# The last list products in a bank of their own, the last sums one place later, and the expert lists in two steps

## The chip, the cores and the metric

One NeuronCore of a Trainium2 chip runs the whole kernel. The metric is the device time in microseconds (us). The kernel before takes 431.78 us, the median of three runs (431.11 to 434.26).

## The reference

The input is a sliding-window attention and the output a mixture of experts on top of it.

```python
# attention: q, k, v of 8 x 8 x 576 x 64, window 64, causal
scores = where(0 <= rel < 64, q @ k.T / 8, -1e9)
x = softmax(scores) @ v          # as 4608 tokens x 512
# mixture of 8 experts, each 512 -> 1024 -> 512
do_compute = x @ w_skip > 0      # the others pass through unchanged
logits = xc @ w_gate             # xc = x[do_compute]
e = argmax(logits); gate = softmax(logits)[e]
out = x;  out[do_compute] = xc + gate * (relu(xc @ w1[e]) @ w2[e])
```

About half the tokens are computed, each by one expert. All arithmetic is in 32-bit floats: matmuls split each operand into a high and a low part and add three products (high x high, and the two mixed ones).

## The kernel before, in words

**The attention part.** The 4608 tokens are 36 tiles of 128. For each tile TensorE makes the scores, VectorE and ScalarE the softmax, TensorE transposes and multiplies by `v`. The logits come out of the same product. `tile_out` (line 782) ends a tile.

**Routing.** Tiles are gathered into five groups (`GRP`, 8, 8, 6, 6 and 8 tiles). For each group the generator `route` (line 507) finds each token's expert, as a one-hot (`gohb`), and its place in that expert's list: the matmuls of lines 515 and 518 make prefix sums in the PSUM tile `pr`, and line 528 adds the running `base`. Then the generator `enter` (line 540) writes the tokens into the lists by matmuls too: `one_hots` (line 576) makes, for each tile, a one-hot of the place inside a list block (`at`, line 601) and a weighted one-hot of the block (line 609), and line 558 multiplies them into `lp`, which line 563 adds to `found`. After the last group `last_entries` (line 672) orders the lists by the size of the experts: a multiplication (line 682) and a sum (line 689) each for the token numbers (c = 0) and the gates (c = 1), then line 691 makes the indices `les`.

**The order of the work** is written by hand, and every engine works its instructions off in that order. Two queues of generators, `late` (of `route`) and `later` (of `enter`), advance by one step at each call of `routes` (line 761). A generator says "sums" ahead of the prefix sums and "lists" ahead of the list products. Behind the last attention tile (`progress[0] == NT`) these steps are held for a number of calls, `HOLD`, so that what they wait for is ready.

**The expert part.** Tokens are worked off in nine items of up to 400 rows, the experts by size. The first two items were gathered early. `expert_chunks` (line 1050) issues a half step of an item at each turn: `up` (product `p`, its high part `hh` by ScalarE, its low part `hl` by VectorE, in two PSUM banks that alternate), and two steps later `down` (into `yw`, `yv` or `yu`). Between them `split_x` (line 879) transposes the next item's rows into the tile `px` and splits them into `xh` and `xl`. `weights_to` (line 850) loads pieces of 512 KB into six buffers (`raw`) and splits them into a high part (`whi`, ScalarE) and a low part (`wlo`, VectorE, line 844), into a ring of nine slots. While routing is not done, it splits only what is needed next; later one piece more at each turn (line 1204).

**The handover.** Behind the last attention tile each turn is: a half step of the experts (`expert_chunk`), one call of `routes`, and, once the last sums are added, one step of `order_experts` (line 1233), which ranks the experts by size. When both queues are empty, each turn may also gather the rows of a further item by POOL's indirect transfers (line 730).

**PSUM banks in the handover.** The pool `late` has four banks: one under the tag "g", two under "w" and one under "u". `pr`, the last `lp` tiles and the `px` tiles all share "g", so each of them waits until the one before it has been read. The bank "u" is used for the first time by the `down` of the fourth item.

Of the kernel before, what the change touches and what calls it, by code (L numbers as in the profile page):

```python
# [8 lines left out]
F32 = mybir.dt.float32  # L9
# [4 lines left out]
ALU = mybir.AluOpType  # L14
# [5 lines left out]
N, D, E, F = 4608, 512, 8, 1024  # L20
P = 128
NB = S // 64
NT = N // P
# [17 lines left out]
NCLOSE = 22  # L41
# [3 lines left out]
NL = E * LT  # L45
# [13 lines left out]
BOTH = 20  # L59
WAIT = {28: 6}  # L60
LWAIT = 8
HOLD = {"sums": 2, "lists": 2}

NXG = 9
CLOSED = 4 * S + 512
# [76 lines left out]
def window_attention_moe(ctx: ExitStack, tc, a, out):  # L142
    nc = tc.nc
# [12 lines left out]
    lists = dram.tile([LROWS, 2], I32, name="lists")  # L156
# [131 lines left out]
    banks = {}  # L288
# [251 lines left out]
    def enter(t0, n):  # L540
        yield
        while t0 >= NCLOSE and progress[0] < NT:
            yield
        parts = [one_hots(t0, n)]
        if t0 + n == NCLOSE:
            parts.insert(0, close_first())
        while parts:
            parts = [z for z in parts if next(z, z) is not z]
            if parts:
                yield  # L550
        at, one = made[0]
        yield "lists"
        if progress[0] < NT:
            lp = banks["av"][:, 0, LAT : LAT + 5 * NL]
        else:
            lp = banks["late"].tile([P, 5 * NL], F32, name="lp", tag="g", bufs=1, padded_shape=[P, 512])
        for j in range(n):
            nc.tensor.matmul(
                lp, at[:, j], one[j // 4][:, j % 4], start=j == 0, stop=j == n - 1, skip_group_check=True
            )  # L560
        yield "listed"
        flat = found.rearrange("p v e j -> p (v e j)")
        nc.vector.tensor_tensor(flat, flat, lp, op=ALU.add)
        if t0 + n == NCLOSE:
            for _ in first_entries():
                yield
            while stores:
                store()
            side.extend(
                (gather_x, xgs[j], es0[:, 0, j // 2, j % 2 : j % 2 + 1], CLOSED) for j in range(4)  # L570
            )
        if t0 + n == NT:
            for _ in last_entries():
                yield

    def one_hots(t0, n):
        g = nc.gpsimd
        here = rows[:, t0 : t0 + n]
        of = xgs[5][:, : n * NL].rearrange("p (n a) -> p n a", a=NL)
        at = xgs[8].bitcast(BF16)[:, : n * P].rearrange("p (n k) -> p n k", k=P)  # L580
        one = [xgs[6 + z].bitcast(BF16)[:, : 4 * 5 * NL].rearrange("p (n v a) -> p n v a", v=5, a=NL) for z in range(2)]
        c = sm.tile([P, n], F32, name="gc")
        g.tensor_scalar(c, here, 1.0 / P, (P / 2 - 0.5) / P, op0=ALU.mult, op1=ALU.subtract)
        g.tensor_scalar(c, c, ROUND, None, op0=ALU.add)
        g.tensor_scalar(c, c, ROUND, float(P), op0=ALU.subtract, op1=ALU.mult)
        k = sm.tile([P, n], F32, name="gk")
        g.tensor_tensor(k, here, c, op=ALU.subtract)
        left = ent[:, t0 : t0 + n, 1]
        for v in (2, 3, 4):
            g.tensor_copy(vals[:, t0 : t0 + n, v], left)  # L590
            if v < 4:
                r = sm.tile([P, n], F32, name=f"gl{v}")
                g.tensor_tensor(r, left, vals[:, t0 : t0 + n, v], op=ALU.subtract)
                left = r
        yield
        tab = cf[:, off["tab"]].unsqueeze(1).to_broadcast([P, n, NL])
        g.tensor_tensor(of, tab, c.unsqueeze(2).to_broadcast([P, n, NL]), op=ALU.subtract)
        g.tensor_scalar(of, of, 0.0, None, op0=ALU.is_equal)
        by = g if t0 < NCLOSE else nc.vector
        for j in range(n):  # L600
            by.tensor_scalar(at[:, j], cf[:, off["iota"]], k[:, j : j + 1], None, op0=ALU.is_equal)
        yield
        for z in range(2):
            m = min(4, n - 4 * z)
            if m > 0:
                r = slice(4 * z, 4 * z + m)
                dims = [P, m, 5, NL]
                v5 = vals[:, t0 + 4 * z : t0 + 4 * z + m]
                g.tensor_tensor(
                    one[z][:, :m], of[:, r].unsqueeze(2).to_broadcast(dims), v5.unsqueeze(3).to_broadcast(dims),  # L610
                    op=ALU.mult,
                )
        made[0] = at, [z.rearrange("p n v a -> p n (v a)") for z in one]
        yield
# [3 lines left out]
    def close_first():  # L618
        g = nc.gpsimd
        key = sm.tile([P, E], F32, name="ckey", bufs=1)  # L620
        cmp = xgs[4][:, : E * E].rearrange("p (i j) -> p i j", i=E)
        rank = sm.tile([P, E], F32, name="crank", bufs=1)
        t1 = sm.tile([P, E], F32, name="ct1", bufs=1)
        g.tensor_scalar(key, base, 16.0, None, op0=ALU.mult)
        g.tensor_tensor(key, key, cf[:, off["kc"]], op=ALU.add)
        g.tensor_tensor(
            cmp,
            key.unsqueeze(1).to_broadcast([P, E, E]),
            key.unsqueeze(2).to_broadcast([P, E, E]),
            op=ALU.subtract,  # L630
        )
        yield
        g.tensor_scalar(cmp, cmp, 0.0, None, op0=ALU.is_gt)
        add_up(rank, cmp, E)
        for j in range(2):
            g.tensor_scalar(first[:, j], rank, float(j), None, op0=ALU.is_equal)
        g.tensor_scalar(t1, rank, 1.5, None, op0=ALU.is_lt)
        g.tensor_tensor(t1, t1, cf[:, off["full"]], op=ALU.mult)
        g.tensor_tensor(t1, t1, base, op=ALU.subtract)
        g.tensor_scalar(t1, t1, 0.0, None, op0=ALU.max)  # L640
        g.tensor_tensor(base, base, t1, op=ALU.add)
        yield
        pl = cmp[:, 0:2]
        m1 = sm.tile([P, 2], F32, name="cm1", bufs=1)
        g.tensor_tensor(pl, first, cf[:, off["e8"]].unsqueeze(1).to_broadcast([P, 2, E]), op=ALU.mult)
        add_up(m1, pl, E)
        g.tensor_scalar(perm, m1, float(NQ * P), None, op0=ALU.mult)
        tables["closed"] = True
# [8 lines left out]
    def first_entries():  # L657
        both = sm.tile([P, 2, E, 2], F32, name="cboth", bufs=1)
        put_together(both, 0, 2)
        yield  # L660
        mine = sm.tile([P, 2, 2, E], F32, name="cmine", bufs=1)
        got = sm.tile([P, 2, 2, 2], F32, name="cgot", bufs=1)
        dims = [P, 2, 2, E]
        for r in range(2):
            is_r = first[:, r].unsqueeze(1).unsqueeze(1).to_broadcast(dims)
            nc.gpsimd.tensor_tensor(mine, both.rearrange("p c e j -> p c j e"), is_r, op=ALU.mult)
            add_up(got[:, r], mine, E)
            yield
        nc.gpsimd.tensor_scalar(es0[:, 0], got[:, :, 0], float(N), None, op0=ALU.add)
        nc.gpsimd.tensor_copy(es0[:, 1].bitcast(F32), got[:, :, 1])  # L670

    def last_entries():
        both = xgs[5][:, : 2 * NL].rearrange("p (c e j) -> p c e j", c=2, j=LT)
        put_together(both, 0, LT)
        yield
        while "order" not in tables:
            yield
        dims = [P, E, LT, E]
        mine = tables["mine"]
        got = tables["got"]  # L680
        for c in range(2):
            nc.vector.tensor_tensor(
                mine,
                both[:, c].rearrange("p e j -> p j e").unsqueeze(1).to_broadcast(dims),
                tables["is"].unsqueeze(2).to_broadcast(dims),
                op=ALU.mult,
            )
            yield
            nc.vector.tensor_reduce(got[:, c], mine, axis=AX.X, op=ALU.add)
            yield  # L690
        nc.vector.tensor_scalar(tables["lists"], got[:, 0], float(N), None, op0=ALU.add)
        for i in range(2, len(ITEMS)):
            its[i].lists(tables["lists"], got[:, 1], ITEMS[i][0], CAP // P if ITEMS[i][0] < 2 else 0)

# [56 lines left out]
    late = []  # L751

    later = []
    held, held2 = [None, 0], [None, 0]
# [6 lines left out]
    def routes(n):  # L761

        for _ in range(n):
            for queue, h in ((late, held), (later, held2)):
                if not queue:
                    continue
                if h[0] in ("sums", "lists"):
                    h[1] += 1
                    if progress[0] < NT or h[1] < HOLD[h[0]] or held[0] == "added":
                        continue  # L770
                step(queue, h)

# [24 lines left out]
    progress = [0]  # L797
# [68 lines left out]
    tables = {}  # L866
# [562 lines left out]
```

## Time and profile before

| | us |
|---|---|
| median of three runs | 431.78 |
| the profiled execution | 432.43 |
| its span in the trace | 430.6 |
| TensorE (PE) busy | 399.1 (93%) |
| VectorE (DVE) busy | 291.2 (68%) |
| ScalarE (ACT) busy | 219.4 (51%) |
| GpSimd (POOL) busy | 157.2 (36%) |

The busy time of an engine counts each of its instructions from start to end, those that overlap once. [...] An idle time stands in brackets behind an instruction, with the instruction that ended it. The handover from attention to experts is at about 160 to 193 us.

### The profile page before, as it was taken

Reading aid. Unit: us, or ns where it says so; the run is one execution under the profiler, and the core shown is the slowest. Engines: PE = TensorE matmul, PEld = TensorE weight load, DVE = VectorE, ACT = ScalarE, POOL = GpSimd, SP = SyncE. Lnnn points to the kernel's source line nnn. Section 1 sums busy time; section 2 is a strip of 40 time slices with the busy share of each in tenths; the row PEclk is TensorE's granted clock in tenths of the full one; section 3 lists DMA queues with packets and bytes.
Section 4 is the critical chain, followed back from the end, with each engine's and each line's share of the span. In section 5 each row is a group of like instructions: output and inputs, shape, how many; then the busy total and the mean of one; then the engine's idle time right before and its main releaser. Section 6 shows DMA issues by size and latency. Waiting matters only on the chain.

```text
span 430.6 us, 11760 instructions
## 1 busy us (share of the span) xinstructions
PE 399.1 (93%) x4673; PEld 330.5 (77%) x4673; DVE 291.2 (68%) x513; ACT 219.4 (51%) x388; POOL 157.2 (36%) x298
## 2 busy tenths in 40 slices
PE   5898999999998977779999899999999999999983
PEld 3576878777786867769898688898887789888662
DVE  3487999889798878779435589475374576756540
ACT  0676787777667675226233445244253444444520
POOL 5211359549679786614304024032043030101011
PEclk9999999999999999899999999999999999999998
DMA  8999999999995984345737827455578675659400
GB/s 271 409 324 329 406 363 376 402 379 294 395 413 158 323 306 149 129 164 187 277 123 243 279 101 266 165 171 179 173 231 279 215 245 193 220 178 300 150 34 20
DMA packets 38840, 105.71 MB, mean 246 GB/s; under 512 B 4896, under 2 KB 6816, under 8 KB 38784
## 3 DMA queue, kind: packets, MB, share of 16 engines
q1 hardware_dynamic: 34160, 93.51, 63.3%
q0 software_dynamic: 3200, 9.58, 6.1%
q10 hardware_dynamic: 1424, 1.85, 1.2%
q8 instruction: 37, 0.61, 0.5%
q14 instruction: 19, 0.16, 0.1%
HBM read 90.86 MB, written 14.39 MB: 244 GB/s over the span
## 4 chain that ended last, share of the span: by engine, by line
PE 76%; DMA 10%; DVE 7%; ACT 3%; POOL 2%; issue 1%; SPq 1%; ACTq 0%; DVEq 0%; POOLq 0%
PE p L908 9%; PE p L910 8%; PE p L909 8%; PE av L386 7%; PE pt L283 6%; PE ps L250 4%; PE yv L908 4%; PE yv L910 3%; PE yv L909 3%; PE yw L908 3%; PE yw L910 3%; DMA vt<-vpt 3%; PE yw L909 3%; DMA q<-qT 3%; DVE wlo L844 2%; PE pw L334 2%
## 5 line engine op out<-in xcount | busy, mean ns | idle before, releaser
L844 DVE TENSOR_TENSOR wlo<-raw,whi 128x1024 fp32r<-128x1024 f32 x70 | 86.2, 1239 | 15.9 <-ACT whi L840 14.0
L954 ACT ACTIVATE hh<-p 128x256 fp32r<-128x256 f32 (+6 forms) x72 | 27.7, 385 | 134.1 <-PE p L910 132.2
L908 PE MATMUL p<-xh,whi 128*128 128x256 f32 (+6 forms) x288 | 85.8, 298 | 0.2 <-ACT xh L886 0.2
L909 PE MATMUL p<-xl,whi 128*128 128x256 f32 (+6 forms) x288 | 84.2, 293 | 0.9 <-DVE xl L889 0.9
L910 PE MATMUL p<-xh,wlo 128*128 128x256 f32 (+6 forms) x288 | 84.2, 292 | 0.0
L957 DVE SCALAR_TENSOR_TENSOR hl<-p,hh 128x256 fp32r<-128x256 f32 (+6 forms) x72 | 30.3, 421 | 67.6 <-ACT hh L954 35.3
L840 ACT CAST whi<-raw 128x1024 fp32r<-128x1024 f32 x72 | 74.5, 1046 | 0.0
L992 POOL DMA_INDIRECT out<-yo,les x18 | 17.6, 976 | 154.6 <-DVE yo L991 151.8
L908 PEld LDWEIGHTS p<-xh,whi 128*128 128x128 f32 x288 | 55.3, 192 | 3.5 <-issue 1.0
L909 PEld LDWEIGHTS p<-xl,whi 128*128 128x128 f32 x288 | 55.3, 192 | 2.2 <-DVE xl L889 1.2
L910 PEld LDWEIGHTS p<-xh,wlo 128*128 128x128 f32 x288 | 55.3, 192 | 0.0
L275 ACT ACTIVATE s<-s 128x1024 f32<-128x1024 f32 x36 | 38.1, 1059 | 25.6 <-DVE s L270 25.5
L269 DVE TENSOR_REDUCE mx<-ps 128x8 f32<-128x1024 f32 x36 | 43.6, 1212 | 8.1 <-PE ps L250 8.1
L270 DVE TENSOR_TENSOR s<-ps,mx 128x1024 f32<-128x1024 f32 x36 | 44.1, 1225 | 5.0 <-ACT vt L371 0.5
L386 PEld LDWEIGHTS av<-vm,ptm 128*64 128x64 f32 x992 | 34.6, 136 | 11.4 <-issue 4.5
L386 PE MATMUL av<-vm,ptm 128*64 128x74 f32 x992 | 39.6, 231 | 2.5 <-POOL vm L355 1.4
L284 ACT COPY ptm<-pt 128x512 f32<-128x512 f32 x72 | 38.2, 581 | 5.7 <-PE pt L283 5.4
L283 PE MATMUL pt<-ident,s 128*128 128x128 f32 x288 | 39.2, 279 | 0.5 <-issue 0.5
L250 PE MATMUL ps<-k,q 64*64 64x128 f32 x1024 | 35.2, 274 | 3.1 <-DMA q<-qT 3.0
L250 PEld LDWEIGHTS ps<-k,q 64*64 64x64 f32 x1024 | 30.9, 136 | 7.0 <-DMA q<-qT 3.4
L283 PEld LDWEIGHTS pt<-ident,s 128*128 128x128 f32 x288 | 30.9, 141 | 3.1 <-issue 0.8
L355 POOL COPY vm<-vm 64x1184 f32<-64x1184 f32 x16 | 18.7, 1166 | 32.1 <-ACT vm L354 28.6
(224 smaller groups left out, 693.9 us busy)
## 6 DMA issues: line engine op xcount, KB each, us to landing
raw<-wq SPq DMA_DIRECT2D x72, 512.0 KB
vm<-vp SPq DMA_DIRECT2D x15, 592.0 KB
vT<-vT SPq DMA_DIRECT2D x16, 512.0 KB
out<-x SPq DMA_DIRECT2D x32, 256.0 KB
q<-qT SPq DMA_DIRECT2D x14, 512.0 KB
wr<-wq SPq DMA_DIRECT2D x24, 256.0 KB
k<-kT SPq DMA_DIRECT2D x7, 640.0 KB
k<-kT SPq DMA_DIRECT2D x7, 512.0 KB
```

What stands on the lines that cost most here:

```text
L250: nc.tensor.matmul(ps[64 * hf : 64 * hf + 64, r, p], q[h, p], k[h, :, p], start=False, stop=p == 3, skip_group_check=True,)
L269: nc.vector.tensor_reduce(mx, flat, axis=AX.X, op=ALU.max)
L270: pace[0] = nc.vector.tensor_tensor(s, flat, mx.unsqueeze(2).to_broadcast([P, 8, P]), op=ALU.subtract)
L275: nc.scalar.activation(s, s, AF.Exp, scale=0.125)
L283: nc.tensor.transpose(pt[:, p], s[:, 4 * r + p], ident)
L284: nc.scalar.copy(ptm[:, 4 * r : 4 * r + 4], pt)
L386: nc.tensor.matmul(av[64 * hf : 64 * hf + 64, h // 4, (h % 4) * VW : (h % 4 + 1) * VW], ptm[:, (h % 2) * 4 + h // 2, 64 * hf : 64 * hf + 6 ...
L840: nc.scalar.copy(ring[n % RING][0], raws[n % NRAW])
L844: by.tensor_tensor(lo, raws[n % NRAW], hi.bitcast(F32), op=ALU.subtract)
L908: nc.tensor.matmul(o, lh, rh, start=first, stop=False)
L909: nc.tensor.matmul(o, lh, rl, start=False, stop=False)
L910: nc.tensor.matmul(o, ll, rh, start=False, stop=last)
```

## The change

`HOLD` for the sums becomes 3. The hold on the lists no longer asks whether the sums have been issued and not added; it lasts one call longer while a route is in the queue `late`. The last `lp` tiles take the tag "u". In `one_hots` the choice of the engine moves into the loop. In `last_entries` the token numbers (c = 0) are multiplied, summed and turned into indices in one step, the gates in the next, where there were five steps.

```diff
-HOLD = {"sums": 2, "lists": 2}
+HOLD = {"sums": 3, "lists": 2}
...
-            lp = banks["late"].tile([P, 5 * NL], F32, name="lp", tag="g", bufs=1, padded_shape=[P, 512])
+            lp = banks["late"].tile([P, 5 * NL], F32, name="lp", tag="u", bufs=1, padded_shape=[P, 512])
...
-        by = g if t0 < NCLOSE else nc.vector
         for j in range(n):
+            by = g if t0 < NCLOSE else nc.vector
             by.tensor_scalar(at[:, j], cf[:, off["iota"]], k[:, j : j + 1], None, op0=ALU.is_equal)
...
-            yield
             nc.vector.tensor_reduce(got[:, c], mine, axis=AX.X, op=ALU.add)
-            yield
-        nc.vector.tensor_scalar(tables["lists"], got[:, 0], float(N), None, op0=ALU.add)
+            if c == 0:
+                nc.vector.tensor_scalar(tables["lists"], got[:, 0], float(N), None, op0=ALU.add)
+                yield
...
-                    if progress[0] < NT or h[1] < HOLD[h[0]] or held[0] == "added":
+                    if progress[0] < NT or h[1] < HOLD[h[0]] + (h is held2 and len(late)):
```

## Rows read from the trace of the kernel before

**Rows 1.** Busy time by stretches: us, each engine's busy us (instructions), clock, DMA share, GB/s.
```profile
160.00:193.00 33.00, 26.04 (x223) 23.73 (x220) 26.26 (x66) 12.17 (x22) 17.90 (x41) 0.95 0.46 152
193.00:400.00 207.00, 205.79 (x1368) 177.33 (x1367) 126.22 (x200) 90.26 (x164) 42.23 (x37) 1.00 0.64 211
```

**Rows 2.** Waits, 160 to 200 us: who waits <- for whom: us, times, longest.
```profile
PE lp L558 <- DVE base L529: 2.9, 1, 2.9
...
PE pr L515 <- DVE gohb L455: 1.7, 1, 1.7
...
PE lp L558 <- DVE xl L889: 1.6, 1, 1.6
...
PE px L885 <- DVE xl L889: 0.8, 1, 0.8
```

**Rows 3.** Timeline of TensorE in the handover: start, us, line, operation, tiles, [idle before <- releaser].
```profile
169.81 0.20 PE L515 MATMUL pr<-gohb,trib 128*128 128x64 bf16 x1 [1.72 <-DVE gohb L455]
...
174.57 0.59 PE L558 MATMUL lp<-xg,xg 128*128 128x160 bf16 x6 [2.85 <-DVE base L529]
...
175.43 0.42 PE L908 MATMUL p<-xh,whi 128*128 128x256 f32 x1
...
178.64 0.34 PE L908 MATMUL p<-xh,whi 128*128 128x256 f32 x1
...
179.41 0.60 PE L885 MATMUL px<-ident,xg 128*128 128x128 f32 x4
...
184.96 0.66 PE L885 MATMUL px<-ident,xg 128*128 128x128 f32 x4 [0.79 <-DVE xl L889]
...
190.06 0.73 PE L558 MATMUL lp<-xg,xg 128*128 128x160 bf16 x8 [1.60 <-DVE xl L889]
...
192.06 0.28 PE L908 MATMUL p<-xh,whi 128*128 128x256 f32 x1
...
193.48 0.28 PE L908 MATMUL p<-xh,whi 128*128 128x256 f32 x1
```

**Rows 4.** Timeline of VectorE in the handover.
```profile
169.10 0.65 DVE L455 SCALAR_TENSOR_TENSOR gohb<-lg,goh 128x64 bf16<-128x64 f32 x1
...
169.99 1.26 DVE L601 TENSOR_SCALAR xg<-cf,gk 128x128 bf16<-128x128 f32 x6
...
171.50 1.22 DVE L844 TENSOR_TENSOR wlo<-raw,whi 128x1024 fp32r<-128x1024 f32 x1
...
173.77 0.42 DVE L957 SCALAR_TENSOR_TENSOR hl<-p,hh 128x256 fp32r<-128x256 f32 x1
...
178.01 0.43 DVE L957 SCALAR_TENSOR_TENSOR hl<-p,hh 128x256 fp32r<-128x256 f32 x1 [2.65 <-ACT hh L954]
...
180.56 2.28 DVE L844 TENSOR_TENSOR wlo<-raw,whi 128x1024 fp32r<-128x1024 f32 x1
...
184.22 0.68 DVE L889 TENSOR_TENSOR xl<-px,xh 128x512 fp32r<-128x512 f32 x1
...
185.15 1.65 DVE L601 TENSOR_SCALAR xg<-cf,gk 128x128 bf16<-128x128 f32 x8
...
189.32 0.69 DVE L889 TENSOR_TENSOR xl<-px,xh 128x512 fp32r<-128x512 f32 x1
```

**Rows 5.** Timeline of POOL: two one-hot products alone, two in the handover, the first gather.
```profile
73.89 2.48 POOL L609 TENSOR_TENSOR xg<-xg,vals 128x640 bf16<-128x640 f32 x2
...
180.12 1.64 POOL L609 TENSOR_TENSOR xg<-xg,vals 128x640 bf16<-128x640 f32 x1
...
181.72 2.24 POOL L609 TENSOR_TENSOR xg<-xg,vals 128x640 bf16<-128x640 f32 x1
...
199.08 1.83 POOL L730 DMA_INDIRECT xg<-out,les  x1 [6.83 <-DVE les L691]
```

**Rows 6.** Two stretches of 2 us each, columns as in the first group.
```profile
138.00:140.00 2.00, 0.57 (x20) 0.55 (x18) 1.02 (x1) 1.32 (x2) 1.86 (x3) 1.00 0.75 194
...
176.00:178.00 2.00, 2.00 (x12) 2.00 (x10) 0.00 (x0) 0.40 (x2) 1.57 (x7) 0.50 0.65 231
```

## The prediction

> **What bounds the kernel now.** I read the busy time by stretches first. The reader is to see that TensorE is full from 193 to 400 us (205.79 of 207 us) and has 6.96 us of idle time in the 33 us from 160 to 193, where the attention part hands over to the experts [rows 1]. So nothing that the change does behind 193 us can gain much by itself, and what it can gain lies in those 33 us. Next the waits of TensorE in that stretch: four of them make 7.0 us, and all four wait for VectorE [rows 2]. The timeline of TensorE says where they stand: ahead of the last sums `pr` (1.72 us), ahead of the first products of one-hots `lp` (2.85 us), ahead of the second transposes `px` (0.79 us) and ahead of the second `lp` (1.60 us) [rows 3]. The timeline of VectorE says why: it has hardly a free moment, with one exception, 2.65 us ahead of the step at 178.01 us, where it waits for an expert product that TensorE could only start after the first `lp` [rows 4]. So the two engines take turns in waiting for each other, and each wait that goes on one shortens the other's.
>
> [...] Fifteen products from 175.43 to 178.64 us take 3.21 us [rows 3]; at full clock twelve of them take 1.42 us (192.06 to 193.48 us), 0.118 us each, so fifteen would take 1.78. The low clock cost 1.43 us.
>
> **The change, part by part.** I call each call of the expert generator a place and count from the first behind the last attention tile. Half steps of the up projection U(q,f) issue at places 1, 2, 4, 5, 7, 8, 12, 13 (q is the quarter, f the half), of item 1 at 17 and 18; the down projection D(q,f) at 9, 10, 14, 15, 19, 20; 3, 6, 11 and 16 are empty.
>
> *The sums wait for three places.* `pr` was issued at place 4 and now is at place 5, behind U(1,1), and its addition on VectorE at place 6. It waits for the one-hot `gohb`, which VectorE has ready at 169.75 us, before and after. U(1,1), 1.42 us, now fills most of the 1.72 us ahead of it.
>
> *The first `lp`* was at place 6 and stays there: its hold is 2 and one more while a route is open, and at place 6 the route has just ended. Only its bank changes. Before, it took the bank of `pr` and had to wait until VectorE had added `pr` to `base`, which stands behind two weight splits of 1.22 us each (171.50 to 173.77 us) and one `hl` [rows 4]: this gives the 2.85 us. In its own bank it waits for the last of six one-hots, which VectorE ends at 171.25 us. Then U(2,0) can begin, but its third product needs the low part of the weights, at about 171.50 + 1.22 = 172.7 us, and ten more products make 173.9 us. U(2,1) needs its product bank back, which `hl` frees at 173.77 + 0.42 = 174.2 us; twelve products end at 175.6 us. The same point, ahead of the first `px`, was at 179.41 us [rows 3]. TensorE is 3.8 us early there.
>
> *VectorE's idle time goes.* U(2,0) ends at 173.9 us, and VectorE is free for its `hl` at 178.01 - 2.65 = 175.36 us, so nothing is waited for and the 2.65 us [rows 4] are gone. All that VectorE does from there up to the second `xl` (end 189.32 + 0.69 = 190.0 us) is the same work in nearly the same order: the ranking of the experts comes one place later throughout, the eight one-hots stay at place 10. So `xl` ends at 190.0 - 2.65 = 187.35 us. TensorE itself, from 175.6 us, needs the 12.65 us between 179.41 and 192.06 without the two waits of 0.79 and 1.60 us: it would be there at 185.9 us. So VectorE decides.
>
> *The second `lp`* keeps place 14 and no longer waits for that `xl`, which held the bank. It needs eight one-hots of VectorE, which end at 186.80 - 2.65 = 184.2 us by the shifted order, and two products of POOL, which end at 183.96 us even if nothing moves them [rows 4, 5]. It and D(1,1), together 2.0 us behind `xl` before (190.06 to 192.06 us), now run ahead of it. The first half step of item 1, U'(0,0), has its second product wait for `xl`: it ends eleven products (1.30 us) behind 187.4 us, at 188.7 us. Before, it ended at 193.48 us [rows 3]. **The gain there is 4.8 us.**
>
> *What is uncertain in it.* VectorE's splits and POOL's one-hots held each other up: the POOL products took 1.64 and 2.24 us where 1.24 is the mean of two alone, and the split 2.28 where 1.22 is usual [rows 4, 5]. With the splits 2 to 3 us earlier this may go (gain 1.06 us more, `xl` at 186.3 us, 5.9 us in all), stay, or fall on the small operations of the ranking, each of which can be held for a whole POOL product: two of 1.24 us, less the 1.06 of the split, make 1.4 us, so 3.4 us in all. I take the middle, the sum with the collisions as they were. [...]
>
> *The lists in two steps.* Two multiplications, two sums and one conversion stay, at places 16 and 17 instead of 16 to 20. They put one sum and the conversion more ahead of `hl` of U'(0,0), both smaller than `xl` and its 0.68 us, so under 1.4 us; that bank is wanted again only after U'(0,1), 1.42 us, and two D steps besides, so nothing on the path. From place 18 instead of 21 POOL may gather and each place may split one weight piece more. The gather waited 6.83 us for the lists [rows 5], and no TensorE wait behind 193 us hangs on it [rows 1], so it is bounded by 0 as gain; without that cover a gather that is late would cost its own length.
>
> *The moved line* `by = ...` inside its loop issues the same instructions: nothing. SP's queue gets the same transfers in the same order; the expert order is read one place later, but earlier in time.
>
> Behind U'(0,0) the 4.8 us can only be kept or given back, since TensorE is full there. The profiled execution took 432.43 us, 1.83 more than its span and 0.65 over the median; I take 4.8 from the median: **427.0 us**.
>
> **The rivals.**
>
> *The gain shrinks in the handover (0.25).* The second `lp` waits for POOL's one-hots, put back by the earlier splits; TensorE idles there and the clock falls. [...] Against it: between 138 and 140 us TensorE was busy for only 0.57 of 2 us, and the clock stayed at 1.00 [rows 6]. Price: 1.4 us for the collisions and 1.43 for the clock, so 2.0 us are left: 429.8 us. [...]
>
> *It is given back later (0.10).* Weight pieces free their slots as items use them; if a load or a slot sets the pace of items 1 and 2, TensorE waits there instead. For it: the transfers run at 211 GB/s in that part [rows 1], not idle. Against it: 1.2 us of idle time in 207. It would be 431.5 us. The same stands for the case that some other dependency holds `lp` at its old time.
>
> *Slower (0.05).* Splits may run ahead from place 18. They stand in VectorE's queue ahead of `hl`; if a piece has not landed, `hl` and the product bank wait. A piece is 128x1024 numbers of 4 bytes, 0.52 MB, 3.4 us at the 152 GB/s of the handover [rows 1]. The first late piece costs less than the gain; it turns to a loss at two in a row (6.9 us), and three (10.3) make 437.3 us. Against it: the same six load buffers fed a full TensorE before [rows 1], and each is now freed earlier too.
>
> **How the numbers follow.** The forecast has 0.60, with 425.8 to 428.4 us as its own range from the bounds of 3.4 and 5.9 us. The range 425.5 to 430.5 us takes in that and nearly all of the first rival, and leaves out the last two. About 1%, 4.3 us, is what a measurement can tell from no change: 427.5 us is the border, half a microsecond above the forecast. Two thirds of the forecast's case lie below it, with a little for gains not thought of: faster 0.46. Slower 0.05, the rest 0.49.
>
> **What would show it.** In the new profile `pr` at about 169.8 us with a wait of under 0.6 us; the first `lp` at about 171.3 us; a granted clock of 1.00 from 174 to 180 us; no VectorE idle time of 2 us near 175 us; the second `lp` ahead of the second `xl`; U'(0,0) ending at 188.7 us, and all later rows early by the same amount. It would be wrong if `lp` still waits for `base`, if the clock falls, or if TensorE idles behind 193 us by more than 1.2 us.

## The result, and the profile after

The changed kernel takes 427.13 us, the median of 20 runs, against 431.52 us for the kernel before, also in 20 runs, of which the first three are those of the table of the kernel before. (A session, below, is a set of runs made together, on one chip.) The ratio is 0.991, with a 95% interval of 0.988 to 0.993. The profiled execution took 428.13 us, with a span of 426.3 us.

In the windows of the changed kernel (columns as in [rows 1]), TensorE is busy for 29.62 of the 33 us of the handover, where it was busy for 26.04.

```profile
160.00:193.00 33.00, 29.62 (x237) 26.60 (x234) 29.58 (x72) 14.20 (x27) 21.04 (x42) 0.95 0.50 161
193.00:400.00 207.00, 206.09 (x1378) 176.88 (x1377) 126.49 (x198) 89.26 (x164) 41.24 (x36) 1.00 0.66 215
...
174.00:176.00 2.00, 2.00 (x12) 2.00 (x11) 1.32 (x7) 0.22 (x1) 0.90 (x4) 0.50 0.78 217
```

The third of them says that the granted clock still falls to 0.50 of the full one, from 174 to 176 us. The waits of TensorE from 160 to 200 us sum to 3.4 us instead of the 7.0 of [rows 2]. `lp` waits neither for `base` nor for `xl`.

```profile
PE p L909 <- DVE xl L889: 1.3, 1, 1.3
PE lp L558 <- DVE xg L601: 1.3, 1, 1.3
PE p L910 <- DVE wlo L844: 0.6, 1, 0.6
PE p L908 <- DVE hl L957: 0.2, 1, 0.2
```

The timeline of TensorE, against [rows 3]. The last line is the last product of U'(0,0).

```profile
169.11 0.20 PE L515 MATMUL pr<-gohb,trib 128*128 128x64 bf16 x1
...
170.80 1.22 PE L558 MATMUL lp<-xg,xg 128*128 128x160 bf16 x6 [1.30 <-DVE xg L601]
...
177.37 0.60 PE L885 MATMUL px<-ident,xg 128*128 128x128 f32 x4
...
182.00 0.60 PE L885 MATMUL px<-ident,xg 128*128 128x128 f32 x4
...
185.28 0.73 PE L558 MATMUL lp<-xg,xg 128*128 128x160 bf16 x8
...
188.90 0.39 PE L909 MATMUL p<-xl,whi 128*128 128x256 f32 x1 [1.34 <-DVE xl L889]
...
190.19 0.28 PE L910 MATMUL p<-xh,wlo 128*128 128x256 f32 x1
```

`pr` waits for nothing, neither does the second `px`, which waited 0.79 us, and the second `lp` stands ahead of the product that needs the second `xl`. The timeline of VectorE, against [rows 4]:

```profile
169.93 1.80 DVE L601 TENSOR_SCALAR xg<-cf,gk 128x128 bf16<-128x128 f32 x6
...
176.20 0.42 DVE L957 SCALAR_TENSOR_TENSOR hl<-p,hh 128x256 fp32r<-128x256 f32 x1 [0.80 <-ACT hh L954]
...
177.13 2.36 DVE L844 TENSOR_TENSOR wlo<-raw,whi 128x1024 fp32r<-128x1024 f32 x2
...
181.42 3.90 DVE L601 TENSOR_SCALAR xg<-cf,gk 128x128 bf16<-128x128 f32 x8
...
188.16 0.68 DVE L889 TENSOR_TENSOR xl<-px,xh 128x512 fp32r<-128x512 f32 x1
```

The idle 2.65 us ahead of `hl` are 0.80, and the pair of weight splits behind it takes 2.36 us. The eight one-hots take 3.90 us instead of 1.65, all the time that POOL multiplies its own, from 182.56 us on (timeline of POOL, against [rows 5]):

```profile
182.56 2.48 POOL L609 TENSOR_TENSOR xg<-xg,vals 128x640 bf16<-128x640 f32 x2
...
191.42 1.51 POOL L730 DMA_INDIRECT xg<-out,les  x1 [0.89 <-DVE les L690]
```

I measure the **handover** from the start of the first product of U(0,0) to the start of the last one of U'(0,0). Before it is 163.51 to 193.36, 29.85 us; in this profile 163.26 to 190.19, 26.93 us. That is 2.9 us less, not 4.8, and another 1.1 us seem to come from behind it (430.6 - 193.36 = 237.24 us are left before, 236.11 after). One place is easy to find there. The timeline of the kernel before has an `hh` that starts 2.4 us after the last of its products (233.69 us, 0.27 us long), a late `xl`, and a wait of TensorE, which the changed kernel's profile doesn't have.

```profile
236.36 0.29 ACT L954 ACTIVATE hh<-p 128x144 fp32r<-128x144 f32 x1 [4.59 <-PE p L910]
...
239.51 0.43 PE L909 MATMUL p<-xl,whi 128*128 128x368 f32 x1 [0.93 <-DVE xl L889]
```

So the total had come out as forecast, with a split that had not. The experiments ask two things: which part of the change carries the gain, and whether those 1.1 us belong to the change at all.

### The profile page after: what moved, and what is told of

Read it like the earlier page. It is cut to its first block, busy times and chain, and to the rows that moved or that the text cites. A ratio compares the mean times of both kernels' runs of the same rounds, so it can differ in the third digit from the quotient of the medians.

```text
span 426.3 us, 11764 instructions
## 1 busy us (share of the span) xinstructions
PE 401.6 (94%) x4673; PEld 332.0 (78%) x4673; DVE 292.1 (69%) x513; ACT 219.6 (52%) x388; POOL 158.4 (37%) x298
## 4 chain that ended last, share of the span: by engine, by line
PE 74%; DMA 8%; DVE 7%; POOL 4%; ACT 3%; issue 2%; SPq 0%; ACTq 0%; DVEq 0%; POOLq 0%
PE p L908 8%; PE p L910 8%; PE p L909 8%; PE av L386 7%; PE pt L283 5%; PE ps L250 5%; PE yv L908 4%; PE yv L910 3%; PE yv L909 3%; DMA vTt<-vTt 3%; DMA wr<-wq 3%; PE yw L908 3%; PE yw L910 3%; PE yw L909 3%; PE pw L334 2%
## 5 line engine op out<-in xcount | busy, mean ns | idle before, releaser
L844 DVE TENSOR_TENSOR wlo<-raw,whi 128x1024 fp32r<-128x1024 f32 x70 | 84.8, 1222 | 15.3 <-ACT whi L840 15.2
L250 PE MATMUL ps<-k,q 64*64 64x128 f32 x1024 | 36.5, 279 | 3.0 <-DMA q<-qT 2.5
L250 PEld LDWEIGHTS ps<-k,q 64*64 64x64 f32 x1024 | 32.0, 138 | 6.8 <-issue 2.4
```

What stands on the lines that cost most here:

```text
L250: nc.tensor.matmul(ps[64 * hf : 64 * hf + 64, r, p], q[h, p], k[h, :, p], start=False, stop=p == 3, skip_group_check=True,)
L844: by.tensor_tensor(lo, raws[n % NRAW], hi.bitcast(F32), op=ALU.subtract)
```

## Experiments

**The bank alone.**

```diff
-  lp = banks["late"].tile([P, 5 * NL], F32, name="lp", tag="g", bufs=1, padded_shape=[P, 512])
+  lp = banks["late"].tile([P, 5 * NL], F32, name="lp", tag="u", bufs=1, padded_shape=[P, 512])
```

> Only the bank: the last lp tiles take the tag u; sums, lists and their holds stay as before, so every engine has the instructions of before in the order of before. Theory (the bank carries the gain): the first lp waits for the six one-hots and not for base, so it starts at about 171.6 us behind U(1,1) instead of 174.6 us, and the second lp no longer waits for xl; the handover is about 3 us shorter and the time about 428.5 us (ratio 0.993, as the whole change). Rival (the later place of the sums carries it): the first lp still starts behind 174 us or the gain is under 1 us, 431 us.

Measured: 429.5 us against 433.94, ratio 0.988 (0.984 to 0.992). The handover is 25.56 us, and the granted clock stays at 1.00. In the timeline the first `lp` waits for nothing, and half of the second waits a little for POOL:

```profile
171.80 0.20 PE L515 MATMUL pr<-gohb,trib 128*128 128x64 bf16 x1 [1.69 <-DVE gohb L455]
...
173.56 0.59 PE L558 MATMUL lp<-xg,xg 128*128 128x160 bf16 x6
...
186.51 0.44 PE L558 MATMUL lp<-xg,xg 128*128 128x160 bf16 x4 [0.38 <-POOL xg L609]
...
189.80 0.39 PE L909 MATMUL p<-xl,whi 128*128 128x256 f32 x1 [1.29 <-DVE xl L889]
```

One word of the change gives all of the gain that can be measured, though `pr` still waits its 1.7 us. The waits of TensorE in the handover sum to 3.70 us (1.69, 0.34, 0.38 and 1.29) against 6.96 before, 3.3 us less. The handover is 4.29 us shorter; an estimate for most of the other 1.0 us is the clock, which was at 0.50 behind the first `lp` before [rows 6] and is not here.

**The holds alone**, with the moved line, which issues the same instructions.

```diff
-HOLD = {"sums": 2, "lists": 2}
+HOLD = {"sums": 3, "lists": 2}
...
-  if progress[0] < NT or h[1] < HOLD[h[0]] or held[0] == "added":
+  if progress[0] < NT or h[1] < HOLD[h[0]] + (h is held2 and len(late)):
```

> Only the holds: sums one place later and the new condition, lp still in the bank of pr and px, lists in five steps. Theory: pr loses its 1.7 us wait, but lp then waits for base to 174.5 us as before and the second lp waits for xl as before: no gain, 431.5 us (ratio 1.000 within 0.003). Rival: 430 us or less, the place alone saves the 1.4 us of the half step that now runs ahead of pr.

Measured: 434.73 us against 433.94, ratio 1.002 (0.999 to 1.004). The wait ahead of `pr` is gone, but the wait ahead of `lp` has grown from the 2.85 us of [rows 3] by 1.06 us:

```profile
172.01 0.20 PE L515 MATMUL pr<-gohb,trib 128*128 128x64 bf16 x1
...
176.31 0.59 PE L558 MATMUL lp<-xg,xg 128*128 128x160 bf16 x6 [3.91 <-DVE base L529]
```

Without the bank, later sums make a later `base`, and `lp` stands behind `base`.

**The lists alone.**

```diff
-            yield
             nc.vector.tensor_reduce(got[:, c], mine, axis=AX.X, op=ALU.add)
-            yield
-        nc.vector.tensor_scalar(tables["lists"], got[:, 0], float(N), None, op0=ALU.add)
+            if c == 0:
+                nc.vector.tensor_scalar(tables["lists"], got[:, 0], float(N), None, op0=ALU.add)
+                yield
```

> Only the lists in two steps; bank and holds as before. Theory: nothing in the handover waits for the lists, so 431.5 us (ratio 1.000 within 0.003). Rival: the weight splits that may run ahead three places earlier, or the earlier gathers, take away waits behind 193 us: 430.3 us, about the 1.1 us that the profile of the changed kernel has less behind the handover.

Measured: 433.95 us against 433.94, ratio 0.999 (0.997 to 1.002). The waits of TensorE are those of before (1.70, 2.85, 0.75 and 1.60 us), and the handover is 29.86 us.

**Bank and holds**, without the lists: the diffs of the first two together.

> Bank and holds, lists in five steps as before. Theory: all of the gain but what the lists give, which is nothing: 427.2 us (ratio 0.991). Rival (the 1.1 us behind the handover belong to the lists): 428.3 us, and the profile shows a TensorE wait of about 1 us for xl behind 230 us again.

Measured: 430.72 us against 433.94, ratio 0.991 (0.988 to 0.995), not to be told from the bank alone. The handover is 25.32 us; the clock stays at 1.00. The timeline shows what now sets its end:

```profile
180.32 2.15 DVE L601 TENSOR_SCALAR xg<-cf,gk 128x128 bf16<-128x128 f32 x8
...
182.94 3.46 POOL L609 TENSOR_TENSOR xg<-xg,vals 128x640 bf16<-128x640 f32 x2
...
183.05 4.43 DVE L844 TENSOR_TENSOR wlo<-raw,whi 128x1024 fp32r<-128x1024 f32 x2
...
186.45 0.44 PE L558 MATMUL lp<-xg,xg 128*128 128x160 bf16 x4 [1.70 <-POOL xg L609]
```

POOL's two products and VectorE's two splits run by turns from 182.9 to 187.5 us, where each pair alone takes 2.5 and 2.35 us. The wait of 0.9 us for `xl` behind 230 us stands here too. That was the sign by which the 1.1 us would belong to the lists; but the lists alone have it as well.

**The changed kernel once more**, in a second session, as the reference for the next three.

> The changed kernel again, unedited, beside the edits below on one chip. Theory (the clock falls by chance in the handover, and the bank alone carries the gain): ratio 0.990 as before; in a second profile the handover, from the first product of U(0,0) to the last of U'(0,0), lies between the 25.3 us of bank and holds with the clock up and the 26.9 us of the first profile. Rival (the lists cost the 1.6 us): 26.9 us again, with the clock at 1.00. Behind the handover: either no TensorE wait for xl near 235 us again (then it belongs to this order of instructions), or the 0.9 us of the five other profiles (then its absence was chance).

Measured: 426.33 us against 431.67, ratio 0.988 (0.984 to 0.992). The handover is 26.73 us, the clock falls to 0.50 from 174 to 176 us, the eight one-hots take 4.28 us, and no wait for `xl` is left behind 195 us.

**One instruction for all one-hots of VectorE**, on the changed kernel.

```diff
-        for j in range(n):
-            by = g if t0 < NCLOSE else nc.vector
-            by.tensor_scalar(at[:, j], cf[:, off["iota"]], k[:, j : j + 1], None, op0=ALU.is_equal)
+        if t0 < NCLOSE:
+            for j in range(n):
+                g.tensor_scalar(at[:, j], cf[:, off["iota"]], k[:, j : j + 1], None, op0=ALU.is_equal)
+        else:
+            nc.vector.tensor_tensor(
+                at, cf[:, off["iota"]].unsqueeze(1).to_broadcast([P, n, P]),
+                k.unsqueeze(2).to_broadcast([P, n, P]), op=ALU.is_equal,
+            )
```

> The change, and the one-hots of the last two groups made by one VectorE instruction each (one tensor_tensor of 6x128 or 8x128 elements) instead of six and eight of 128. Theory (each VectorE instruction there is held for a whole POOL instruction): one instruction can be held once, so it takes about 1.2 us of work and at most 1.26 us of waiting where eight took 3.9 us; the second xl ends 1.4 to 2.5 us earlier, the 1.34 us wait of U'(0,0) for it goes, and the time is about 1.5 us under the change, ratio 0.987. Rival (the eight are slow by themselves or the path is elsewhere): less than 0.5 us.

Measured: 426.98 us against 431.67, ratio 0.990 (0.986 to 0.994), so no gain on the changed kernel (0.988) where 1.5 us had been expected. The handover is 26.08 us, 0.65 less than in the changed kernel beside it, with the clock at 0.50 from 174 to 176 us in both. The one-hots are short now, and the second half of `lp` waits for POOL instead:

```profile
181.10 1.21 DVE L603 TENSOR_TENSOR xg<-cf,gk 128x1024 bf16<-128x1024 f32 x1
...
186.63 0.44 PE L558 MATMUL lp<-xg,xg 128*128 128x160 bf16 x4 [1.17 <-POOL xg L614]
```

**The kernel before with the bank and that one instruction**, without holds and lists.

> The kernel before with only the bank changed, and the one-hots by one instruction each. Theory: the holds and the lists give nothing, so this is as fast as the change with the one instruction, ratio 0.987, within 0.003 of it. Rival: 2 us slower than that, because the half step ahead of pr counts once VectorE is faster.

Measured: 427.52 us against 431.67, ratio 0.992 (0.988 to 0.995). The second `xl` starts as early as 183.11 us, and still the handover is 27.76 us: both halves of `lp` wait for POOL, in turn.

```profile
183.11 0.68 DVE L894 TENSOR_TENSOR xl<-px,xh 128x512 fp32r<-128x512 f32 x1
184.36 0.44 PE L558 MATMUL lp<-xg,xg 128*128 128x160 bf16 x4 [1.85 <-POOL xg L614]
...
185.57 0.69 PE L558 MATMUL lp<-xg,xg 128*128 128x160 bf16 x4 [0.78 <-POOL xg L614]
```

The windows (columns as in [rows 1]) show that the clock falls behind the first of these waits:

```profile
185.00:188.00 3.00, 2.43 (x9) 2.04 (x9) 0.94 (x2) 0.00 (x0) 1.41 (x4) 0.50 0.46 156
```

The handover is 1.68 us longer than with holds and lists, as the rival had it; in the total (0.992 against 0.990) the two cannot be told apart.

**Eight filler products** behind `pr` in the changed kernel, which do nothing but keep TensorE busy.

```diff
+        if t0 + n == NT:
+            idle = banks["late"].tile([P, 512], F32, name="idle", tag="u", bufs=1)
+            for _ in range(8):
+                nc.tensor.matmul(
+                    idle, identb, band[:, 0].unsqueeze(1).to_broadcast([P, 4, P]),
+                    start=True, stop=True, skip_group_check=True,
+                )
```

> The change, and eight more matmuls of 128x128 by 128x512 behind pr, into the bank of lp, whose result nobody reads: they fill some 1.7 us of the wait ahead of the first lp. Theory (the low clock in the handover follows TensorE's wait there): the clock stays at 1.00 from 172 to 178 us, the fifteen or so slow products take 1.3 us less, and since VectorE waits for them (0.80 us idle before hl) 0.5 to 1.3 us of it reach the end: ratio 0.988. Rival: the clock falls all the same, or VectorE sets the pace alone: within 0.3 us of the change.

Measured: 427.35 us against 431.67, ratio 0.990 (0.987 to 0.993). The windows show the clock at 1.00 where it was 0.50:

```profile
174.00:176.00 2.00, 1.99 (x16) 1.79 (x16) 1.93 (x8) 0.78 (x2) 0.57 (x2) 1.00 0.59 170
```

The handover is 26.05 us, 0.7 less than in the changed kernel beside it, and the total shows nothing of it. One profile does not show that the fillers kept the clock up: further down the changed kernel keeps it without them in one of three profiles. The mean granted clock of whole executions hints at it, with 0.991 to 0.998 in the twelve runs with fillers and 0.987 to 0.995 in the six of the changed kernel beside them.

**Less work for POOL.** In the last set of one-hots POOL multiplies two of the five value columns; the columns of the gates are left out, so the gates aren't those of the reference.

```diff
-                dims = [P, m, 5, NL]
-                v5 = vals[:, t0 + 4 * z : t0 + 4 * z + m]
+                w = 2 if t0 + n == NT else 5
+                dims = [P, m, w, NL]
+                v5 = vals[:, t0 + 4 * z : t0 + 4 * z + m, :w]
```

> The changed kernel, but for the last set of eight tiles POOL multiplies the one-hots by two of the five value columns only (the token number); the gate columns keep older numbers, so the gates are not those of the reference. POOL's two products cost 2.48 us in the changed kernel, of 640 columns each; 256 columns should cost about half. If VectorE and POOL hold each other up and this sets the end of the handover: the eight one-hots on VectorE fall from 3.90 us to at most 3.0, the second lp no longer waits, the second xl ends by 187.5 us less the shift of the run, and the handover (first product start of U(0,0) to last product start of U'(0,0)) falls from 26.93 to 26.0 us or less; time 0.5 to 1.5 us under the changed kernel, ratio about 0.988. Rival, VectorE's own work sets the end: the eight one-hots fall, but the xl behind them ends as before and the handover stays at 26.7 to 27.

Measured: 428.07 us against 433.25, ratio 0.990 (0.987 to 0.993). The eight one-hots take 2.15 us, the second `xl` ends at 187.41 us, and the handover is 24.08 us, the shortest of all. The second `lp` still waits a little:

```profile
183.55 2.18 POOL L610 TENSOR_TENSOR xg<-xg,vals 128x256 bf16<-128x256 f32 x2
183.66 3.15 DVE L845 TENSOR_TENSOR wlo<-raw,whi 128x1024 fp32r<-128x1024 f32 x2
...
185.78 0.44 PE L558 MATMUL lp<-xg,xg 128*128 128x160 bf16 x4 [0.41 <-POOL xg L610]
```

The wait of `lp` was expected to go, and 0.41 us of it are left. No profile of the changed kernel stands beside this one. Against bank and holds, a profile of the same kind (the table below), the handover is 1.24 us shorter, so the theory that the turns of POOL and VectorE set the end holds for the handover. In the total I had expected 0.5 to 1.5 us; the ratio can't show that much.

**Bank and lists**, without the holds, in the same session.

> The bank and the lists, without the holds. What it tells apart: whether the 0.9 us that TensorE waits for xl behind 195 us (there before, with the bank alone, the holds alone, the lists alone, and bank and holds; gone with the whole change) goes with the lists once the bank is there. If the lists with the bank remove it: no xl wait behind 195 us, hh of U(2,3) starts when its own products end (idle of about 2.2 us instead of 4.6). If it needs all three: the wait of 0.9 us stands. The holds are worth nothing by the earlier run: ratio 0.988 to 0.992 either way, sums wait 1.7 us, first lp without a wait for base, handover 25.5 to 27.5 us.

Measured: 429.22 us against 433.25, ratio 0.990 (0.987 to 0.994). The handover is 24.63 us, less than expected, and `pr` waits 0.78 us instead of 1.7; the reason stands below the table. The wait for `xl` behind 195 us stands. But so it does in the kernel with less work for POOL, which has all three parts of the change. So the three parts of the change, which the first profile of the changed kernel had without the wait, don't decide it. That made a new theory: it goes with the session.

**Both kernels unchanged, in one session.** The last two runs.

> The kernel before, unchanged, profiled in the same call as the changed kernel. Two theories of the TensorE wait of 0.9 us for xl behind 195 us, which the profile of before shows and that of the changed kernel does not. By the first it belongs to the kernel: it stands here, with hh of U(2,3) idle for about 4.7 us, and gohb ends about 6.2 us behind the first product of U(0,0). By the second it belongs to the session of runs (it was absent in all four kernels of one call, present in all six of two others): it is present or absent here as in the changed kernel beside it, and where it is absent gohb ends about 5.4 us behind the first product. Ratio 1.000, 0.997 to 1.003 either way.

> The changed kernel, unchanged, beside the kernel before. If the session decides, the xl wait behind 195 us and the place of gohb are as in the kernel before of this call, and the whole gain of 3.5 to 5 us stands in the handover, between the first product of U(0,0) and the last of U'(0,0). If the kernel decides, the wait is absent here and present there, and the handover gives about 3 us of the gain. Ratio 0.988 to 0.991.

Measured: the kernel before 431.58 us, ratio 0.999 (0.996 to 1.002); the changed kernel 426.33 us against 431.8, ratio 0.988 (0.982 to 0.994). The timeline of the kernel before in that last session has its `hh` as the products end, and no wait of TensorE for `xl` behind 195 us is left, though nothing was changed in it. In the handover its first `lp` waits longer than in [rows 3]:

```profile
164.06 0.39 PE L908 MATMUL p<-xh,whi 128*128 128x256 f32 x1
...
175.86 0.98 PE L558 MATMUL lp<-xg,xg 128*128 128x160 bf16 x6 [4.46 <-DVE base L529]
...
191.72 0.73 PE L558 MATMUL lp<-xg,xg 128*128 128x160 bf16 x8 [1.60 <-DVE xl L889]
...
195.04 0.28 PE L910 MATMUL p<-xh,wlo 128*128 128x256 f32 x1
...
235.69 0.29 ACT L954 ACTIVATE hh<-p 128x144 fp32r<-128x144 f32 x1 [2.23 <-PE p L910]
```

Its windows show a long stretch at the low clock, and the timeline of VectorE the splits at the ranking of the experts:

```profile
176.00:182.00 6.00, 6.00 (x31) 6.00 (x30) 2.58 (x9) 2.26 (x3) 4.90 (x16) 0.50 0.40 135
...
181.09 3.42 DVE L844 TENSOR_TENSOR wlo<-raw,whi 128x1024 fp32r<-128x1024 f32 x2
```

The timeline of the changed kernel beside it:

```profile
163.04 0.38 PE L908 MATMUL p<-xh,whi 128*128 128x256 f32 x1
...
170.59 1.22 PE L558 MATMUL lp<-xg,xg 128*128 128x160 bf16 x6 [1.30 <-DVE xg L601]
...
175.94 2.36 DVE L844 TENSOR_TENSOR wlo<-raw,whi 128x1024 fp32r<-128x1024 f32 x2
...
179.95 2.15 DVE L601 TENSOR_SCALAR xg<-cf,gk 128x128 bf16<-128x128 f32 x8
...
182.58 3.46 POOL L609 TENSOR_TENSOR xg<-xg,vals 128x640 bf16<-128x640 f32 x2
...
182.69 4.43 DVE L844 TENSOR_TENSOR wlo<-raw,whi 128x1024 fp32r<-128x1024 f32 x2
...
186.09 0.44 PE L558 MATMUL lp<-xg,xg 128*128 128x160 bf16 x4 [1.69 <-POOL xg L609]
...
187.04 0.68 DVE L889 TENSOR_TENSOR xl<-px,xh 128x512 fp32r<-128x512 f32 x1
...
189.12 0.28 PE L910 MATMUL p<-xh,wlo 128*128 128x256 f32 x1
```

The handover is 30.98 us before and 26.08 after, so 4.90 us less. Behind it 430.3 - 195.04 = 235.26 us are left before, and 424.4 - 189.12 = 235.28 after: nothing is won or lost there. The 4.90 us are favoured by the clock: here it stays at 1.00 in the changed kernel, and in the kernel before it is at 0.50 from 176 to 182 us, where the first profile of that kernel had 0.77 on average. (The other 1.02 us between these two executions lie ahead of U(0,0), where the kernels are the same.)

All profiled executions, sorted by whether TensorE waits for `xl` behind 195 us; "left" is the span less the end of the handover, the last column the median of the kernel before beside it:

| kernel | handover | left | `xl` wait | before, us |
|---|---|---|---|---|
| before (shown first) | 29.85 | 237.24 | 0.93 | |
| bank alone | 25.56 | 236.80 | 0.9 | 433.94 |
| holds alone | 29.82 | 236.92 | 0.9 | 433.94 |
| lists alone | 29.86 | 236.83 | 0.9 | 433.94 |
| bank and holds | 25.32 | 236.92 | 0.93 | 433.94 |
| less work for POOL | 24.08 | 236.78 | 0.9 | 433.25 |
| bank and lists | 24.63 | 236.74 | 0.9 | 433.25 |
| changed (shown first) | 26.93 | 236.11 | none | 431.52 |
| changed, second session | 26.73 | 235.18 | none | 431.67 |
| one instruction | 26.08 | 235.23 | none | 431.67 |
| bank, one instruction | 27.76 | 235.45 | none | 431.67 |
| filler products | 26.05 | 236.41 | none | 431.67 |
| before, last session | 30.98 | 235.26 | none | 431.80 |
| changed, last session | 26.08 | 235.28 | none | 431.80 |

The 237.24, 236.11 and 236.41 us hold waits of TensorE for a transfer (`wr`) of 0.5, 0.8 and 1.0 us. Two of these handovers began late and look short for that: with the holds alone and with bank and lists, the last transposes of the attention part took 1.89 and 1.80 us instead of 1.09. From the end of `gohb` to the end of the handover the holds alone take 24.49 us against 23.61 before, bank and lists 19.33 against 19.35 with the bank alone, and less work for POOL 17.83.

## Why the prediction was right

427.0 us were forecast from a median of 431.78 and 427.13 were measured. It was right in the mechanism and nearly so in the size. In the handover 4.8 us were forecast. The changed kernel's three profiles, against the kernel before of the last session, give 4.05, 4.25 and 4.90; bank and holds against [rows 3], both of the other kind, give 4.53 (29.85 - 25.32). That the 4.90 and the total come so near the forecast is in part luck. The forecast handover was 25.05 us (29.85 - 4.8), and the changed kernel took 26.08 to 26.93; the 4.90 were measured from a kernel before that itself took 30.98. The medians of the changed kernel lie 4.4 to 5.5 us below those beside them. The two first profiles, 2.9 us apart in the handover, are of different kinds, and the 1.1 us behind it go with the kind, not with the change.

*The sums.* Right: `pr` lost its wait. But by itself that was worth nothing, as the holds alone show: the wait moves to `lp`. With the bank it isn't measurable either (0.988 without the holds, 0.991 with them, intervals that overlap).

*The bank.* Right, and the carrier of all of the gain that can be measured. The first `lp` was forecast for 171.3 us, 7.8 us behind the first product of U(0,0); it came 7.5 us behind it (170.59 - 163.04). The first `px` was to come 12.1 us behind it (175.6 - 163.51); with bank and holds it came 12.24 us behind, in the last session 13.00, and in the first profile, with the clock down, 14.11.

*The idle time of VectorE.* Right in the main: I had nothing left of the 2.65 us, and 0.80 are left in the first profile. The second `xl` was to end 23.84 us behind the first product (187.35 - 163.51); with bank and holds it ended 23.93 us behind it (188.09 - 164.16), in the last session 24.68 (187.72 - 163.04), and in the first profile of the changed kernel 25.58 (188.84 - 163.26).

*The collisions.* I took the sum of them as it was, and that is about what came, though not one of them stayed where it was. In the last session the early ones went: the splits at the ranking took 3.42 us before and 2.36 after, two small operations 0.42 and 0.94 before and 0.23 and 0.21 after, 1.98 us in all. Late ones came: the eight one-hots 2.15 instead of 1.65 us, the splits behind them 4.43 instead of 2.35, 2.58 us in all. So the net loss is 0.6 us, inside the bounds of +1.06 and -1.4.

*The second `lp`.* Half wrong. It did go ahead of the second `xl`, but I let POOL end its products at 183.96 us at the latest. POOL started later, not earlier: in the last session two of its small operations were held for about 1 us each by VectorE's splits. Then split and products started together and took turns, and POOL ended at 182.58 + 3.46 = 186.04 us; half of `lp` waited 1.69 us for that. It cost little, since `xl`, held up by the same turns, ended at 187.72 us.

*The clock.* I expected 1.00 from 174 to 180 us. In two of three profiled executions of the changed kernel it fell to 0.50 behind the first `lp`, in the third it stayed at 1.00. Where it stayed, alone or by the filler products, the handover took 26.08 and 26.05 us; where it fell, 26.93 and 26.73. So the executions with the fall are 0.65 to 0.88 us longer, other collisions included; I had put 1.43 on it. That was TensorE's loss on fifteen products, and about as many ran slow here too (in the first profile from 173.24 us on, 0.21 us apart), but less than that reached the end of the handover. In the runs the clock fell behind waits of TensorE (2.85 us before, 1.30 us here, to 0.50 in both) and stayed at 1.00 in the one profile where filler products stood in the wait. They don't say why it fell behind the same wait of 1.30 us in two executions and not in a third; that the wait brings the fall was not shown.

*The first rival* came true in pieces that did not meet. POOL was late and the second `lp` waited 1.69 us for it in the last session, but the clock stayed at 1.00. The clock fell in the other two profiles, behind the first `lp`, where TensorE waited for VectorE's one-hots, and there the second `lp` had no wait. A fall behind the wait of the second `lp` came only in the kernel with the bank and the one instruction (0.50 from 185 to 188 us). The price in the changed kernel was 0.7 to 0.9 us of clock and 0.6 us of collisions, not 2.8.

*Lists and the moved line.* Right: the lists alone give a ratio of 0.999, and the gather that they bring forward to 191.42 us had nobody waiting for it. The slower rival left no trace: behind the handover the two kernels of the last session take the same time to 0.02 us.

**What stays open.** What differs between the sessions isn't found. In sessions of one kind ScalarE's `hh` starts as its own products end, in the other 2.4 us later, about when the third product of the next `yw` ends; the kernel before is 1.5 to 2.4 us slower in those, by the medians of the table. The first profile of the kernel before doesn't fit that: it has the late `hh`, but the three runs reported with it have a median of 431.78. The kinds differ ahead of the handover as well: in the profiles with the late `hh`, ScalarE also starts a copy of the attention part (`ptm`, line 284) 1.2 us later, and TensorE waits 1.5 us for it instead of 0.29. Two sessions on the same chip were of different kinds, so it isn't the chip alone. And a version better than the changed one wasn't found: both edits that relieved VectorE alone passed the wait on to POOL. Taking POOL's products off it whole, without leaving work out, wasn't tried.

## What to carry to other kernels

Where two engines wait for each other through a shared PSUM bank, look for the tile that needn't share it: here its own bank was worth 4.3 us in the handover and 4.4 in the median, while moving the wait by reordering was worth nothing. Before a difference between two profiles is put down to a change, profile both kernels in one session: here 1.1 us of the first comparison went with the kind of the session. And profile each kernel more than once: by the pair taken, the gain in the handover came out as 2.9 to 4.9 us, in part because the clock fell to 0.50 in some executions and not in others (0.65 to 0.88 us). Where VectorE and POOL hold each other up, look at both: here relieving VectorE alone handed the wait to POOL (1.17 us of `lp`), and less work for POOL shortened the handover (24.08 us against 25.32 with bank and holds).

## What the runs showed of the hardware

The eight one-hots of VectorE are of one tensor each and a scalar per partition, 0.2 us apiece (1.65 us for eight), and take 3.90 to 4.34 us while POOL multiplies two tensors. In the first profile of the changed kernel, even an addition on 128x8 numbers (`gs`, line 458) took 1.24 us under the POOL product at 168.72 us, where it takes 0.17 in the first profile of the kernel before. The other way round, POOL's operations on 128x8 numbers, 0.2 to 0.3 us each, took 1.26 and 1.12 us in the last session while VectorE split weights. So these three were held for 0.85 to 1.07 us each (1.24 - 0.17 = 1.07 for `gs`, 1.26 - 0.20 and 1.12 - 0.27 for POOL's two), and two of the three, `gs` and POOL's 1.12 us (`gc`), have one tensor input.

In [rows 4] and [rows 5] the holds go by turns, one instruction each: POOL's first product there ends at 181.76 us; VectorE's split, begun before that, ends at 182.84, 1.08 us behind it, and POOL's second product, begun before that, at 183.96, 1.12 us behind the split. With bank and holds POOL's two products took 3.46 us from 182.94 us on and VectorE's two splits 4.43 from 183.05 on: together 4.54 us, nearly the sum of 2.48 and 2.35 us that the pairs take alone. Eight short instructions of VectorE beside two long ones of POOL lose 2.3 to 2.7 us (3.90 - 1.65 and 4.34 - 1.65), and two long splits beside the same two lose about 2 (4.43 - 2.35 = 2.08). The one instruction for all eight (1.21 us, from 181.10 us) was over before POOL's products began at 183.12 us; the turns fell to the splits behind it.
